# Attention with a softplus layer behind it on one core: in batches 3 to 7 the output matmuls stand two tiles behind h, and sums are placed and split otherwise

## The chip, the cores and the metric

The kernel runs on one core of a Trainium2 chip. The metric is the device time of one execution in microseconds (us). Three runs of the kernel before gave 1178.12, 1180.25 and 1180.36 us; the median is 1180.25 us. A further execution was profiled; the traces and tables here come from it. Engine names in the profile: PE is TensorE (matmuls; PEld are its weight loads), DVE is VectorE, ACT is ScalarE, POOL is GpSimd, SP is SyncE, which issues the DMAs.

## The reference

Eight batches of eight heads; 512 local and 32 global positions of 64 numbers each. A local position attends to the 32 global keys and to local keys within 32 positions; a global position attends to all 544 keys. The rows that come out are the input of a two-layer network with softplus between the layers:

```
s_g = scale * q_g @ concat(k_g, k_l)^T;   out_g = softmax(s_g) @ concat(v_g, v_l)
s_ll = where(|i - j| <= 32, scale * q_l @ k_l^T, -1e9);   s_lg = scale * q_l @ k_g^T
out_l = softmax(concat(s_lg, s_ll)) @ concat(v_g, v_l)
x = concat(out_g, out_l) as (8 * 544, 512)
h = x @ w_in                                   # 512 x 2048
g = max(h, 0) + log1p(exp(-|h|))
out = g @ w_out                                # 2048 x 512
```

All of it is fp32. Each of the two big products is made as three matmuls of rounded high parts and low remainders (high by high, low by high, high by low).

## The kernel before

**Attention.** Work goes by m, a pair of heads (m = 0 to 31, four to a batch). m = 0 to 5 are done ahead of everything, with a scheme of their own. For each m from 6 on there are: `scores` (PE, then DVE adds the mask and `block_maxima` takes maxima of 32 by 32 blocks); `maxima` (`fold` brings four partition groups together with POOL copies, reduces on DVE and copies, then three copies spread the result); `probs`, in two halves (DVE transposes the maxima, POOL subtracts them at L387, ACT takes the exponential at L389, DVE sums blocks at L393); `totals` (`fold` again, reciprocal, three copies, a transpose at L404); `values` (PE) and `normalise` (DVE), which leave x of four m in the tiles xa[b, 0..3]. From m = 9 (`WIDE`) on, `both_scores` does both halves of the scores together: one in the PSUM tile a, the other in both banks of the pool ps_h.

**Batches 0 to 2.** The tile f (16 of them) is 128 of the 2048 columns of h for 512 rows: `hpart` makes h (12 matmuls for the tile, in two parts), `act` makes g (three ACT instructions, e at L695 on DVE, the rounded gh at L698 on ACT, the remainder gl at L700 on POOL), `opart` adds g's product with w_out to the four PSUM banks o0 to o3. Batch 0 shares its time with the weights: they are loaded as 64-bit numbers and split by ACT, DVE and POOL (L575 to L594).

**Batches 3 to 7** (`FAST` = 3) make h by a scheme with seven products where the plain one has eight. It needs sums of blocks of w_in: `mix` makes them once, 16 in all, on POOL (L475, L476), DVE (L477, L479) and ACT (L478), and sends them to a DRAM scratch, from which `load_ring` brings them back in a ring of 12 tiles. It needs sums of blocks of x: `sums_x(b)` makes them on POOL, 14 instructions, and `operand_x(b, i)` splits operand i into high and low (ACT and DVE). A pair p (p = 0 to 7) makes the tiles p and p + 8 of h: `six(b, p)` does six products (36 matmuls) into two PSUM banks of ps_h (in the last batch odd p take the tile a), copying parts to the tile c with ACT; L677 on DVE forms the first h and `act(b, p)` follows; `seventh(b, p)` does the last product (six matmuls), L686 forms the second h, `act(b, p + 8)` follows. `product` frees a ring tile behind odd p, and in pair 7 it calls operand_x for the next batch behind each product. gh and gl have three buffers each, e has two, ps_h two banks.

**What sets the order.** `moe_items` writes a list of items; in batches 3 to 7 a pair stands there as: six, half a tile of o, seventh, half a tile of o, act of the second tile, scores if p is even, a whole tile of o. The o are those of the last tile of the pair before and of the first tile of this pair: o stands one tile behind h. `pieces` gives the attention work slots in units of which a batch has 48; the main loop calls a piece when the items done have reached its slot. Matmuls stay in the order of this program, by `mm`'s chain; the other engines' instructions are put in order by the framework's scheduler, which goes by when it reckons that each is ready. Waits between engines go by semaphores, and each engine runs its own queue in order.

Of the kernel before, what the change touches and what calls it, by code (L numbers as in the profile page):

```python
# [8 lines left out]
F32 = mybir.dt.float32  # L9
# [4 lines left out]
ALU = mybir.AluOpType  # L14
# [5 lines left out]
P = 128  # L20
# [44 lines left out]
def moe_over_global_local_attention(  # L65
# [290 lines left out]

    def fold(t, op):

        for a in range(1, 4):
            nc.gpsimd.tensor_copy(t[0:32, GW * a:GW * a + GW], t[32 * a:32 * a + 32, 0:GW])  # L362
        e0 = 4 * GW
        for u, du, off in ((0, 1, -2), (3, 1, 3)):
            nc.vector.tensor_reduce(grid(t, e0 + u, (7, 6), (du, 2)), grid(t, 3 + u, (12, 6), (du, 2), (off, 2), (GW, 4)), axis=AX.XY, op=op)
        nc.vector.tensor_reduce(grid(t, e0 + 2, (7, 6), (4, 2)), grid(t, 3 + 2, (12, 6), (7, 2), (GW, 4)), axis=AX.X, op=op)
        g = e0 + 44
        nc.vector.tensor_reduce(grid(t, g, (1, 2)), grid(t, 3 + 5, (36, 2), (12, 3), (3, 2), (GW, 4)), axis=AX.XYZ, op=op)
        nc.vector.tensor_copy(grid(t, e0 + 5, (21, 2), (7, 3)), t[0:32, g:g + 2].unsqueeze(2).to_broadcast([32, 2, 3]))
        return t[:, e0:e0 + 44]  # L370

    def maxima(m):
        e = fold(st.pop(("mt", m)), ALU.max)
        for a in range(1, 4):
            i = nc.vector.tensor_copy(e[32 * a:32 * a + 32, 0:42], e[0:32, 0:42]).ins  # L375
        order["maxima"] = i
        st["e", m] = e

    def probs(m, g):
# [14 lines left out]
                                axis=AX.X, op=ALU.add, apply_transpose=True)  # L394

    def totals(m):
        e = fold(st.pop(("zt", m)), ALU.add)
        nc.vector.tensor_scalar(e[0:32, 0:42], e[0:32, 0:42], 1e-9, None, op0=ALU.add)
        nc.vector.reciprocal(e[0:32, 0:42], e[0:32, 0:42])
        for a in (2, 3, 1):  # L400
            o = 21 * (a // 2)
            nc.vector.tensor_copy(e[32 * a:32 * a + 32, 0:21], e[0:32, o:o + 21])
        rb = st["rb", m] = pl.tile([P, 640], F32, tag="rb", name=f"rb{m}", bufs=1)
        nc.vector.transpose(rb.rearrange("p (s k) -> p s k", k=32), e[:, 0:20].unsqueeze(2).to_broadcast([P, 20, 32]))  # L404

# [27 lines left out]
    def pieces():  # L433
        def piece(*fs):
            def go():
                for f in fs:
                    f()
            return go
        ps = []
        for m in range(M0, M):  # L440
            soon = (5, 11.5, 14.7) if m <= 4 * FAST + 4 else (3, 9.5, 13)
            g0, g1, mx, tot, val = SLOTS.get(m, (None, None) + tuple(12 * m + u for u in soon))
            for g, slot in ((0, g0), (1, g1)) if m in SLOTS else ():
                fs = [lambda m=m, g=g: scores(m, g)]
                if m + 1 < M:
                    fs += [lambda m=m, p=p: load(m + 1, p) for p in ((0,), (1, 2))[g]]
                ps.append((slot, piece(*fs)))
            ps.append((mx, piece(lambda m=m: maxima(m), *[lambda m=m, q=q: probs(m, q) for q in range(2)])))
            ps.append((tot, lambda m=m: totals(m)))
            fs = [lambda m=m: values(m), lambda m=m: normalise(m)]  # L450
            if m + 2 < M:
                fs.append(lambda m=m: load_v(m + 2))
            ps.append((val, piece(*fs)))
        for i in range(16):
            ps.append((MIX0 + MIX1 * i, lambda i=i: (mix_out(i), mix(*MIXES[i]))))
        ps.sort(key=lambda t: t[0])
        return ps
# [9 lines left out]
    def mix(q, what):  # L467

        t = mixed
        a11, a12, a21, a22 = wi[2 * q], wi[2 * q + 1], wi[2 * q + 8], wi[2 * q + 9]  # L470
        x, y, op = {"S3": (a11, a21, ALU.subtract), "S1": (a21, a22, ALU.add),
                    "S2": (t.get("S1"), a11, ALU.subtract), "S4": (a12, t.get("S2"), ALU.subtract)}[what]
        o = t[what] = pl.tile([P, 2, 512], F32R, tag="cv", name=f"mix{q}{what}", bufs=2)
        lo = o[:, 1].bitcast(F32)
        nc.gpsimd.tensor_tensor(o[:, 0].bitcast(F32), x[:, 0].bitcast(F32), y[:, 0].bitcast(F32), op=op)  # L475
        nc.gpsimd.tensor_tensor(lo, x[:, 1].bitcast(F32), y[:, 1].bitcast(F32), op=op)  # L476
        nc.vector.tensor_tensor(lo, lo, o[:, 0].bitcast(F32), op=ALU.add)  # L477
        nc.scalar.copy(o[:, 0], lo)  # L478
        nc.vector.tensor_tensor(o[:, 1], lo, o[:, 0].bitcast(F32), op=ALU.subtract)  # L479
# [15 lines left out]
    SECOND = ((lambda t: t[:, 0:128].unsqueeze(1), 0, 1, 128), (lambda t: windows(t, 288, 224, 2, 64), 128, 2, 64))  # L495
    sums, xs = {}, {}

    def sums_x(b):
        t13 = pl.tile([P, 2, 2, 256], F32, tag="cv", name=f"t13_{b}", bufs=2)
        t24 = pl.tile([P, 2, 2, 256], F32, tag="cv", name=f"t24_{b}", bufs=2)  # L500
        t1, t3, t2, t4 = t13[:, 0], t13[:, 1], t24[:, 0], t24[:, 1]
        assert all((b, j) in ready for j in range(4))
        lower, upper = [xa[b, 0], xa[b, 1]], [xa[b, 2], xa[b, 3]]
        for k in range(2):
            cut = lambda t, o, n, w: t[:, k, o:o + n * w].rearrange("p (n w) -> p n w", n=n)
            for f, o, n, w in SECOND:
                a = windows(lower[k], 160 if o == 0 else 384, w, n, w)
                nc.gpsimd.tensor_tensor(cut(t1, o, n, w), f(lower[k]), a, op=ALU.subtract)
                nc.gpsimd.tensor_tensor(cut(t2, o, n, w), f(upper[k]), cut(t1, o, n, w), op=ALU.subtract)  # L509
                nc.gpsimd.tensor_tensor(cut(t3, o, n, w), f(upper[k]), f(lower[k]), op=ALU.subtract)  # L510
            nc.gpsimd.tensor_tensor(cut(t4, 0, 2, 128), half_1(upper[k]), cut(t2, 0, 2, 128), op=ALU.subtract)  # L511
        sums[b] = {5: t1, 6: t2, 7: t3, 4: t4}
# [95 lines left out]
    def moe_items():  # L608
# [46 lines left out]

        def six(b, p):

            if b == B - 1 and p % 2:
                t = ps_a.tile([P, 2, 512], F32, tag="a", name=f"h{b}_{p}")
                t = [t[:, 0], t[:, 1]]  # L660
            else:
                t = [ps_h.tile([P, 512], F32, tag="h", name=f"h{b}_{p}_{u}") for u in range(2)]
            X, N, Q, V = t[0][:, 0:256], t[0][:, 256:512], t[1][:, 0:256], t[1][:, 256:512]
            if "c" not in g:
                g["c"] = pl.tile([P, 2, 512], F32, tag="wi3", name="c", bufs=1)
            c = g["c"]
# [10 lines left out]
            nc.vector.tensor_tensor(c[:, 0], t[1], c[:, 0], op=ALU.add)  # L677
# [70 lines left out]
        for i, (b, f) in enumerate(tiles):  # L748
            if f == 0 and b > 0 and not FAST <= b < B:
                items.append((b, 0, 0, lambda b=b: [split_x(b, j) for j in range(4)]))  # L750
            if FAST <= b < B:
                if f < 8:
                    if f == 7 and b < B - 1:
                        items.append((b, 0, 0, lambda b=b: sums_x(b + 1)))
                    items.append((b, 6, 0, lambda b=b, f=f: six(b, f)))
                    second(done, b)
                    items.append((b, 1, 0, lambda b=b, f=f: seventh(b, f)))
                    second(done + 1, b)
                    items.append((b, 0, 0, lambda b=b, f=f: act(b, f + 8)))
                    m = next(wide, None) if f % 2 == 0 else None  # L760
                    if m:
                        items.append((b, 0, 0, lambda m=m: both_scores(m)))
                    second(done + 2, b)
                    second(done + 3, b)
                    done += 4
                continue
            if 0 < b < B - 1:
                if f == 0:
                    h = iter(range(NF))
                    for what in ORDER:  # L770
                        if what == "H":
# [3 lines left out]
                            if b == FAST - 1 and f % 2 and f > 4:  # L775
                                items.append((b, 0, 0, lambda f=f: (load_ring(f - 5), load_ring(f - 4))))
                            if b == FAST - 1 and f == NF - 1:
                                items.append((b, 0, 0, lambda b=b: sums_x(b + 1)))
                                items.append((b, 0, 0, lambda b=b: [operand_x(b + 1, i) for i in range(7)]))
                        elif what == "O":  # L780
                            second(done, b)
# [175 lines left out]
```

## Time and profile before

| | us |
|---|---|
| median of three runs | 1180.25 |
| the profiled execution | 1181.58 |
| its span, first to last instruction | 1179.80 |
| busy: PE / DVE / ACT / POOL | 994.3 / 760.4 / 567.2 / 550.2 |
| PE idle ahead of o from gh, ended by gh | 96.6 |
| mean granted clock of PE | 0.927 |

Busy times are the union of an engine's instructions; PE's ends are modelled, so that neighbouring matmuls overlap a little in the records, and the price of a step on PE is best read from start to start. "Idle before" is the time in which the engine did nothing ahead of an instruction, with the instruction that ended it. A row of the windows view holds: start:end, length, the busy time of PE, PEld, DVE, ACT and POOL with instruction counts, PE's granted clock (1 is full), the DMA engines' share and GB/s. In the timeline a row holds start, length, engine, line, operation, output and inputs, count, and the idle time ahead of it in brackets. In the waits view a row holds who waited, for whom, total us, times, longest.

Batch 0's h starts at 85 us; the following batches 1 and 2 run to 447 us. The pairs of batch 4 run from 591.7 to 731.5 us, those of batch 5 to 871.4, those of batch 6 to 1004.7, those of batch 7 to 1122.2; the last 58 us are the rows of the global positions.

### The profile page before, as it was taken

To read this page: it belongs to the slowest core of one execution; us is meant where nothing else is said; L and a number is where in the kernel's file an instruction comes from. 1 tells how busy PE (TensorE), PEld (TensorE's weight loads), DVE (VectorE), ACT (ScalarE), POOL (GpSimd) and SP (SyncE) were. 2 spreads that over 40 slices of the span, in tenths; PEclk is the share of its full clock that TensorE was granted. 3 is DMA by queue.
4 is the path that set the end of the run, shared out by engine and by line. 5 is a ranking of instruction groups with operands and counts; after the bars stand their busy time and mean duration, and the time that the engine had idled before them with its cause. 6 is when DMAs were issued, how large, how long until landed. Compare 5 with 4: busy or idle time off the path is not lost. (4 is left out here: it accounts for less than half of the span.)

```text
span 1179.8 us, 16894 instructions
## 1 busy us (share of the span) xinstructions
PE 994.3 (84%) x5955; PEld 810.1 (69%) x5959; DVE 760.4 (64%) x1427; ACT 567.2 (48%) x1086; POOL 550.2 (47%) x736
## 2 busy tenths in 40 slices
PE   6888977789999998888689886888978878788898
PEld 4676755567777787776578765667757666666687
DVE  6889698896676778656876557766675674221211
ACT  6777554544444463443543444444454345444443
POOL 5768889774444453434534334443343452111121
PEclk8999999799999998988899888899888889998999
DMA  9944433331122343344453333544334433433330
GB/s 357 358 148 160 177 97 118 126 112 41 41 79 88 122 152 105 139 154 151 166 201 104 122 134 139 202 166 149 105 137 143 166 126 143 161 125 113 118 127 19
DMA packets 61493, 164.95 MB, mean 140 GB/s; under 512 B 10720, under 2 KB 14560, under 8 KB 61408
## 3 DMA queue, kind: packets, MB, share of 16 engines
q1 hardware_dynamic: 60592, 163.77, 39.6%
q8 instruction: 47, 0.77, 0.3%
q14 instruction: 38, 0.31, 0.1%
q10 hardware_dynamic: 816, 0.10, 0.1%
HBM read 137.63 MB, written 26.21 MB: 139 GB/s over the span
## 5 line engine op out<-in xcount | busy, mean ns | idle before, releaser
L133 PE MATMUL o<-wo,gh 128*128 128x512 f32 x1088 | 383.5, 436 | 100.8 <-ACT gh L698 96.6
L700 POOL TENSOR_TENSOR gl<-e,gh 128x512 fp32r<-128x512 f32 (+1 forms) x152 | 189.0, 1248 | 389.7 <-ACT gh L698 381.7
L133 PEld LDWEIGHTS o<-wo,gh 128*128 128x128 f32 x1088 | 217.6, 210 | 155.8 <-ACT gh L698 108.4
L133 PE MATMUL o<-wo,gl 128*128 128x512 f32 x544 | 239.8, 441 | 31.5 <-POOL gl L700 31.0
L133 PEld LDWEIGHTS o<-wo,gl 128*128 128x128 f32 x544 | 113.8, 209 | 79.4 <-POOL gl L700 53.8
L387 POOL TENSOR_TENSOR s<-s,mb 128x320 f32<-128x320 f32 (+6 forms) x136 | 143.2, 1086 | 49.5 <-DVE mb L383 47.5
L133 PE MATMUL h<-xh,ring 128*128 128x256 f32 x768 | 141.4, 285 | 4.6 <-ACT c L671 2.3
L133 PE MATMUL h<-xh,wi 128*128 128x512 f32 x384 | 122.8, 401 | 12.0 <-DVE e L695 10.8
L133 PEld LDWEIGHTS h<-xh,ring 128*128 128x128 f32 x768 | 122.4, 192 | 11.9 <-ACT c L671 3.1
L698 ACT CAST gh<-e 128x512 fp32r<-128x512 f32 x136 | 83.4, 613 | 89.8 <-DVE e L695 88.3
L677 DVE TENSOR_TENSOR c<-h,c 128x512 f32<-128x512 f32 x40 | 27.0, 676 | 132.2 <-PE h L133 132.2
L133 PE MATMUL h<-xl,ring 128*128 128x256 f32 x384 | 107.5, 280 | 0.0
L133 PE MATMUL h<-x,ring 128*128 128x256 f32 x720 | 99.8, 282 | 6.5 <-ACT c L675 6.3
L133 PEld LDWEIGHTS h<-x,ring 128*128 128x128 f32 x720 | 93.2, 188 | 12.5 <-ACT c L675 8.5
L694 ACT ACTIVATE e<-e,one 128x512 f32<-128x512 f32 x136 | 97.7, 719 | 2.1
L133 PEld LDWEIGHTS h<-xh,wi 128*128 128x128 f32 x384 | 72.2, 191 | 32.3 <-DVE e L695 14.2
L668 ACT COPY c<-h 128x256 f32<-128x256 f32 x40 | 14.9, 371 | 161.4 <-PE h L133 161.4
L393 DVE TRANSPOSE_TENSOR_REDUCE zt<-s 128x32 f32<-128x1024 f32 x52 | 64.6, 1242 | 41.6 <-ACT s L389 41.5
L693 ACT ACTIVATE e<-e 128x512 f32<-128x512 f32 x136 | 85.4, 628 | 2.6
L695 DVE SCALAR_TENSOR_TENSOR e<-c,e 128x512 f32<-128x512 f32 x80 | 64.8, 810 | 26.8 <-ACT e L694 23.9
L692 ACT ACTIVATE e<-c 128x512 f32<-128x512 f32 x80 | 50.2, 628 | 59.3 <-DVE c L677 54.9
L133 PE MATMUL h<-xl,wi 128*128 128x512 f32 x192 | 76.2, 397 | 0.0
(193 smaller groups left out, 1607.4 us busy)
## 6 DMA issues: line engine op xcount, KB each, us to landing
ring<-mix_scratch SPq DMA_DIRECT2D x156, 512.0 KB, 5.7
raw<-in_qk SPq DMA_DIRECT2D x52, 272.0 KB, 3.0
v<-in_v SPq DMA_DIRECT2D x26, 384.0 KB, 3.1
wiraw<-in_w_in SPq DMA_DIRECT2D x16, 512.0 KB, 9.0
woraw<-in_w_out SPq DMA_DIRECT2D x16, 512.0 KB, 9.0
mix_scratch<-wi SPq DMA_DIRECT2D x16, 512.0 KB, 5.4
out<-ot SPq DMA_DIRECT2D x29, 256.0 KB, 2.1
raw<-in_qk SPq DMA_DIRECT2D x26, 224.0 KB, 3.4
```

What stands on the lines that cost most here:

```text
L133: order["pe"] = after(nc.tensor.matmul(*a, **k), "pe").ins
L387: nc.gpsimd.tensor_tensor(s[:, h, o:o + w], s[:, h, o:o + w], mb[:, h, q:q + w], op=ALU.subtract)
L393: nc.vector.tensor_reduce(windows(st["zt", m], 4 + 16 * g, 36, 2, 16), s.rearrange("p h (b k) -> p h b k", k=32), axis=AX.X, op=ALU.add, a ...
L668: nc.scalar.copy(c[:, 0, 0:256], X)
L677: nc.vector.tensor_tensor(c[:, 0], t[1], c[:, 0], op=ALU.add)
L692: nc.scalar.activation(e, ph, AF.Abs)
L693: nc.scalar.activation(e, e, AF.Exp, scale=-1.0)
L694: nc.scalar.activation(e, e, AF.Ln, bias=one)
L695: nc.vector.scalar_tensor_tensor(e, ph, 0.0, e, op0=ALU.max, op1=ALU.add)
L698: nc.scalar.copy(gh, e)
L700: nc.gpsimd.tensor_tensor(gl[:, c], e[:, c], gh[:, c].bitcast(F32), op=ALU.subtract)
```

## The change

In batches 3 to 7 a pair becomes: six, half a tile of o, seventh, half a tile of o, act of the second tile, scores if p is even, a whole tile of o, where the o are now those of both tiles of the pair before. `sums_x` makes half of its sums ahead of pair 6, half ahead of pair 7. In the last batch all pairs use ps_h. The second half of `probs` has a slot of its own, 1.5 later, for m over 16, and the slots of the m that are divisible by four lie later. In `mix` two additions go from DVE to POOL, and the slots of its 16 calls begin later and lie closer together. The small copies of `fold`, `maxima` and `totals` go from DVE to ACT for m = 6, 7 and 8, and the splitting of the weights is no longer ordered behind the maxima of those m. e (L695) stays on DVE.

```diff
-MIX0, MIX1 = 104, 4
+MIX0, MIX1 = 110, 3.6
...
+    def small(m):
+        return nc.scalar.copy if m < WIDE else nc.vector.tensor_copy
...
-        nc.vector.tensor_copy(grid(t, e0 + 5, (21, 2), (7, 3)), t[0:32, g:g + 2].unsqueeze(2).to_broadcast([32, 2, 3]))
+        small(m)(grid(t, e0 + 5, (21, 2), (7, 3)), t[0:32, g:g + 2].unsqueeze(2).to_broadcast([32, 2, 3]))
...
         for a in range(1, 4):
-            i = nc.vector.tensor_copy(e[32 * a:32 * a + 32, 0:42], e[0:32, 0:42]).ins
-        order["maxima"] = i
+            i = small(m)(e[32 * a:32 * a + 32, 0:42], e[0:32, 0:42]).ins
+        if m >= WIDE:
+            order["maxima"] = i
...
-            nc.vector.tensor_copy(e[32 * a:32 * a + 32, 0:21], e[0:32, o:o + 21])
+            small(m)(e[32 * a:32 * a + 32, 0:21], e[0:32, o:o + 21])
...
-            soon = (5, 11.5, 14.7) if m <= 4 * FAST + 4 else (3, 9.5, 13)
+            soon = (5, 11.5, 14.7) if m <= 4 * FAST + 4 else (3, 9.5, 13) if m % 4 else (7, 13, 16)
...
-            ps.append((mx, piece(lambda m=m: maxima(m), *[lambda m=m, q=q: probs(m, q) for q in range(2)])))
+            ps.append((mx, piece(lambda m=m: maxima(m), lambda m=m: probs(m, 0))))
+            ps.append((mx + (1.5 if m > 4 * FAST + 4 else 0), lambda m=m: probs(m, 1)))
...
-        nc.vector.tensor_tensor(lo, lo, o[:, 0].bitcast(F32), op=ALU.add)
+        nc.gpsimd.tensor_tensor(lo, lo, o[:, 0].bitcast(F32), op=ALU.add)
         nc.scalar.copy(o[:, 0], lo)
-        nc.vector.tensor_tensor(o[:, 1], lo, o[:, 0].bitcast(F32), op=ALU.subtract)
+        nc.gpsimd.tensor_tensor(o[:, 1], lo, o[:, 0].bitcast(F32), op=ALU.subtract)
...
-    def sums_x(b):
+    def sums_x(b, k):
...
-        for k in range(2):
-            cut = lambda t, o, n, w: t[:, k, o:o + n * w].rearrange("p (n w) -> p n w", n=n)
-            for f, o, n, w in SECOND:
-                a = windows(lower[k], 160 if o == 0 else 384, w, n, w)
+        lower, upper = xa[b, k], xa[b, k + 2]
+        cut = lambda t, o, n, w: t[:, k, o:o + n * w].rearrange("p (n w) -> p n w", n=n)
+        for f, o, n, w in SECOND:
+            a = windows(lower, 160 if o == 0 else 384, w, n, w)
...
-            if b == B - 1 and p % 2:
-                t = ps_a.tile([P, 2, 512], F32, tag="a", name=f"h{b}_{p}")
-                t = [t[:, 0], t[:, 1]]
-            else:
-                t = [ps_h.tile([P, 512], F32, tag="h", name=f"h{b}_{p}_{u}") for u in range(2)]
+            t = [ps_h.tile([P, 512], F32, tag="h", name=f"h{b}_{p}_{u}") for u in range(2)]
...
-                    if f == 7 and b < B - 1:
-                        items.append((b, 0, 0, lambda b=b: sums_x(b + 1)))
+                    if f in (6, 7) and b < B - 1:
+                        items.append((b, 0, 0, lambda b=b, k=f - 6: sums_x(b + 1, k)))
                     items.append((b, 6, 0, lambda b=b, f=f: six(b, f)))
-                    second(done, b)
-                    items.append((b, 1, 0, lambda b=b, f=f: seventh(b, f)))
-                    second(done + 1, b)
-                    items.append((b, 0, 0, lambda b=b, f=f: act(b, f + 8)))
-                    m = next(wide, None) if f % 2 == 0 else None
-                    if m:
-                        items.append((b, 0, 0, lambda m=m: both_scores(m)))
-                    second(done + 2, b)
-                    second(done + 3, b)
-                    done += 4
+                    late = 2 * tiles.index((b, f)) - done
+                    assert late == 4 or (b, f) == (FAST, 0) and late <= 4, (b, f, late)
+                    k = iter(range(done, done + late))
+                    for step in "OHOAGOO":
+                        if step == "O":
+                            k0 = next(k, None)
+                            if k0 is not None:
+                                second(k0, b)
+                                done += 1
+                        elif step == "H":
+                            items.append((b, 1, 0, lambda b=b, f=f: seventh(b, f)))
+                        elif step == "A":
+                            items.append((b, 0, 0, lambda b=b, f=f: act(b, f + 8)))
+                        elif f % 2 == 0:
+                            m = next(wide, None)
+                            if m:
+                                items.append((b, 0, 0, lambda m=m: both_scores(m)))
```

`second(i, b)` puts half a tile of o, the i-th of the list, into the items.

More of the change, by code (lines that the diff above doesn't have):

```diff
@@ L355, in grid, with fold @@
         return bass.AP(base.tensor, base.offset, [list(base.ap[0])] + [list(d) for d in dims])
-    def fold(t, op):
+    def small(m):
+        return nc.scalar.copy if m < WIDE else nc.vector.tensor_copy
+    def fold(t, op, m):
         for a in range(1, 4):
@@ L368, in fold @@
         nc.vector.tensor_reduce(grid(t, g, (1, 2)), grid(t, 3 + 5, (36, 2), (12, 3), (3, 2), (GW, 4)), axis=AX.XYZ, op=op)
-        nc.vector.tensor_copy(grid(t, e0 + 5, (21, 2), (7, 3)), t[0:32, g:g + 2].unsqueeze(2).to_broadcast([32, 2, 3]))
+        small(m)(grid(t, e0 + 5, (21, 2), (7, 3)), t[0:32, g:g + 2].unsqueeze(2).to_broadcast([32, 2, 3]))
         return t[:, e0:e0 + 44]
     def maxima(m):
-        e = fold(st.pop(("mt", m)), ALU.max)
+        e = fold(st.pop(("mt", m)), ALU.max, m)
         for a in range(1, 4):
-            i = nc.vector.tensor_copy(e[32 * a:32 * a + 32, 0:42], e[0:32, 0:42]).ins
-        order["maxima"] = i
+            i = small(m)(e[32 * a:32 * a + 32, 0:42], e[0:32, 0:42]).ins
+        if m >= WIDE:
+            order["maxima"] = i
         st["e", m] = e
@@ L396, in totals @@
     def totals(m):
-        e = fold(st.pop(("zt", m)), ALU.add)
+        e = fold(st.pop(("zt", m)), ALU.add, m)
         nc.vector.tensor_scalar(e[0:32, 0:42], e[0:32, 0:42], 1e-9, None, op0=ALU.add)
@@ L496, in moe_over_global_local_attention @@
     sums, xs = {}, {}
-    def sums_x(b):
[L499 to L503, printed above, removed]
-        for k in range(2):
-            cut = lambda t, o, n, w: t[:, k, o:o + n * w].rearrange("p (n w) -> p n w", n=n)
-            for f, o, n, w in SECOND:
-                a = windows(lower[k], 160 if o == 0 else 384, w, n, w)
[L508 to L512, printed above, removed]
+    def sums_x(b, k):
+        if k == 0:
+            t13, t24 = (pl.tile([P, 2, 2, 256], F32, tag="cv", name=f"{n}_{b}", bufs=2) for n in ("t13", "t24"))
+            sums[b] = {5: t13[:, 0], 6: t24[:, 0], 7: t13[:, 1], 4: t24[:, 1]}
+        t1, t2, t3, t4 = (sums[b][i] for i in (5, 6, 7, 4))
+        assert (b, k) in ready and (b, k + 2) in ready
+        lower, upper = xa[b, k], xa[b, k + 2]
+        cut = lambda t, o, n, w: t[:, k, o:o + n * w].rearrange("p (n w) -> p n w", n=n)
+        for f, o, n, w in SECOND:
+            a = windows(lower, 160 if o == 0 else 384, w, n, w)
+            nc.gpsimd.tensor_tensor(cut(t1, o, n, w), f(lower), a, op=ALU.subtract)
+            nc.gpsimd.tensor_tensor(cut(t2, o, n, w), f(upper), cut(t1, o, n, w), op=ALU.subtract)
+            nc.gpsimd.tensor_tensor(cut(t3, o, n, w), f(upper), f(lower), op=ALU.subtract)
+        nc.gpsimd.tensor_tensor(cut(t4, 0, 2, 128), half_1(upper), cut(t2, 0, 2, 128), op=ALU.subtract)
     def operand_x(b, i):
@@ L777, in moe_items @@
                             if b == FAST - 1 and f == NF - 1:
-                                items.append((b, 0, 0, lambda b=b: sums_x(b + 1)))
+                                items.append((b, 0, 0, lambda b=b: [sums_x(b + 1, k) for k in range(2)]))
                                 items.append((b, 0, 0, lambda b=b: [operand_x(b + 1, i) for i in range(7)]))
```

## The prediction

> **What bounds the kernel now.** I read the page first, for the tile that TensorE (PE) idles in front of; then the busy times by stage, to see where that idling lies; then the waits of one batch and TensorE's timeline, for its price.
>
> ```profile
> PE 994.3 (84%) x5955; PEld 810.1 (69%) x5959; DVE 760.4 (64%) x1427; ACT 567.2 (48%) x1086; POOL 550.2 (47%) x736
> L133 PE MATMUL o<-wo,gh 128*128 128x512 f32 x1088 | 383.5, 436 | 100.8 <-ACT gh L698 96.6
> ```
>
> PE is the busiest engine, and 100.8 us of idle time stand ahead of one group, the output matmuls o, which wait for gh, the softplus of h rounded by ScalarE (ACT). By stage (the columns are PE, PE's weight loads, VectorE = DVE, ACT, GpSimd = POOL, then PE's granted clock): five rows are batches 3 to 7, one each; the last two are batch 0 and batch 1.
>
> ```profile
> 451.00:591.70 140.70, 113.10 (x705) 93.48 (x705) 100.19 (x203) 63.46 (x118) 64.84 (x91) 0.88 0.42 147
> 591.70:731.50 139.80, 114.67 (x738) 95.19 (x738) 93.78 (x187) 62.11 (x118) 58.47 (x82) 0.89 0.42 148
> 731.50:871.40 139.90, 114.63 (x738) 95.21 (x737) 93.73 (x187) 62.13 (x118) 58.47 (x82) 0.89 0.43 148
> 871.40:1004.70 133.30, 111.34 (x709) 92.75 (x708) 77.82 (x157) 60.03 (x116) 49.64 (x68) 0.91 0.40 141
> 1004.70:1122.20 117.50, 94.59 (x518) 77.50 (x516) 28.59 (x37) 52.88 (x101) 17.93 (x14) 0.94 0.38 133
> 85.00:195.00 110.00, 95.74 (x440) 73.07 (x444) 94.46 (x142) 64.76 (x108) 96.29 (x109) 0.97 0.43 154
> 195.00:321.00 126.00, 103.60 (x534) 81.84 (x529) 98.92 (x176) 54.74 (x87) 76.28 (x88) 0.93 0.23 81
> ```
>
> In batches 3 to 7 nothing is full: PE is busy 115 of 140 us at a clock of 0.89, DVE 94. So it is a chain of latencies. The waits of batch 4 (window 591.7 to 731.5) name it: the four gh waits end with PE idle, the next four are DVE's own.
>
> ```profile
> PE o L133 <- ACT gh L698: 21.5, 4, 7.8
> DVE c L677 <- PE h L133: 17.8, 4, 4.9
> PE o L133 <- POOL gl L700: 2.4, 4, 0.6
> DVE zt L365 <- POOL zt L362: 6.8, 4, 2.0
> DVE zt L393 <- ACT s L389: 5.1, 6, 1.3
> DVE mt L365 <- POOL mt L362: 3.8, 4, 1.0
> DVE e L695 <- ACT e L694: 2.0, 6, 0.4
> ```
>
> PE's timeline through two pairs of that batch (start, length) gives the price of every step:
>
> ```profile
> 652.60 1.22 PE L133 MATMUL o<-wo,gh 128*128 128x512 f32 x2 [4.28 <-ACT gh L698]
> ...
> 658.90 0.63 PE L133 MATMUL h<-xh,ring 128*128 128x256 f32 x2
> ...
> 664.79 0.86 PE L133 MATMUL h<-x,ring 128*128 128x256 f32 x6
> 665.49 0.62 PE L133 MATMUL o<-wo,gh 128*128 128x512 f32 x2
> ...
> 666.98 2.21 PE L133 MATMUL s_ps<-raw 64*128 64x160 f32 x28
> 669.11 0.73 PE L133 MATMUL o<-wo,gh 128*128 128x512 f32 x2
> ...
> 672.20 1.96 PE L133 MATMUL v_ps<-s,v 128*64 128x160 f32 x24
> 674.09 0.51 PE L133 MATMUL h<-xh,ring 128*128 128x256 f32 x2
> ...
> 678.45 0.63 PE L133 MATMUL o<-wo,gh 128*128 128x512 f32 x2
> ...
> 679.85 0.39 PE L133 MATMUL h<-x,ring 128*128 128x256 f32 x2
> ```
>
> From start to start: six() 4.36 us (674.09 to 678.45), half a tile of o 1.40 (678.45 to 679.85), seventh() 0.70 (664.79 to 665.49), scores 2.13 (666.98 to 669.11), a whole tile of o behind them 3.09, values 1.89. The tile of o at 652.60 took 6.30 us to the start of six() at 658.90: after a 4.28 us gap its matmuls run at half pace (two in 1.22 us against 0.62). Less its gl wait of about 0.6, that is 5.7 against 2.8, so 2.9 us lost on top of the gap.
>
> **The change, part by part.** *o two tiles behind h (batches 3 to 7).* Before, o of the tile that six() made comes after half an o, seventh() and half an o: 1.40 + 0.70 + 1.40 = 3.5 us (more with scores and values). Now a whole tile of o and the next six() lie between as well: 3.5 + 2.8 + 4.36 = 10.65 us, and 14.7 in pairs with scores and values. The same count of matmuls is issued; only their order moves. What must fit is the time from six()'s end until gl is written:
>
> ```profile
> 1009.22 0.69 DVE L677 TENSOR_TENSOR c<-h,c 128x512 f32<-128x512 f32 x1 [9.66 <-PE h L133]
> ...
> 1014.53 1.28 POOL L700 TENSOR_TENSOR gl<-e,gh 128x512 fp32r<-128x512 f32 x1 [12.61 <-ACT gh L698]
> ```
>
> ```profile
> 687.08 1.79 POOL L700 TENSOR_TENSOR gl<-e,gh 128x512 fp32r<-128x512 f32 x1 [2.76 <-ACT gh L698]
> ```
>
> ```profile
> 712.92 0.63 PE L133 MATMUL o<-wo,gh 128*128 128x512 f32 x2
> ...
> 725.83 1.28 POOL L700 TENSOR_TENSOR gl<-e,gh 128x512 fp32r<-128x512 f32 x1 [4.03 <-ACT gh L698]
> ```
>
> Without attention around it (batch 7) the chain takes 1014.53 + 1.28 - 1009.22 = 6.6 us, hidden. In a pair without scores it took 687.08 + 1.79 - 678.45 = 10.4, because maxima and probs stand ahead on DVE and ACT: just hidden. At the end of a batch (operand_x for the next one in the way) 727.11 - 712.92 = 14.2: about 3.5 us stay open. Three gh buffers suffice: when seventh()'s gh is written, the oldest tile's o has been issued.
>
> If PE alone decides, two pairs take 2 x (4.36 + 0.70) + 4 x 1.40 + 3.09 + 2.8 + 2.13 + 1.89 = 25.6 us, a batch 102.5. The other way: 139.8 - 21.5 - 2.4 - 4 x 2.9 = 104.3. So about 103.
>
> What is late next is DVE. Its 93.8 us of work in batch 4 stay (e stays there too), and it runs in order. Its waits for PE go when PE runs ahead; those for POOL and ACT, 6.8 + 5.1 + 3.8 + 2.0 = 17.7, I keep whole, though probs' second half, moved 1.5 slots later, may shorten them. That makes 111.5, more than 103, so DVE sets batches 3 to 5: 100.2 + 17.7 = 117.9, 111.5 and 111.4, a gain of 22.8 + 28.3 + 28.5. Batch 6 has three scores left: DVE 77.8 + 3/4 of 17.7 = 91, PE 3 x 25.6 + 2 x 10.65 = 98.1, plus 3.5 at the boundary = 101.6: 31.7 gained. Batch 7 has none: 8 x 10.65 + 3.5 = 88.7 against 117.5: 28.8. ACT (52.9 of 88.7) is not full.
>
> *The clock.* The forecast lets the short waits that DVE imposes cost nothing beyond themselves. This row pair of batch 7 speaks against that:
>
> ```profile
> 1027.50:1031.00 3.50, 1.87 (x7) 0.87 (x6) 1.58 (x3) 2.96 (x5) 1.05 (x1) 1.00 1.00 408
> 1031.00:1034.50 3.50, 3.22 (x8) 2.55 (x9) 0.77 (x1) 0.62 (x1) 1.50 (x2) 0.56 0.03 11
> ```
>
> PE was busy 1.87 of 3.50 us, with no gap as long as 1.7, and the clock of the next 3.5 us was 0.56. So two short gaps close together can cost up to 1.5 us more. If that happened once in every two pairs of batches 3 to 6, it would be 16 x 1.5 = 24 us; I keep it for the range. [...]
>
> *sums_x split.* Its 14 instructions for a batch stay; half go ahead of the pair 6, half ahead of pair 7. POOL is busy 58 of 140 us: nothing, and with 112 it still has room.
>
> *The scores' 4th map later; the last batch's odd h in ps_h.* The first takes DVE work out of the boundary, inside the 3.5 us that I left there. The second lets six() of batch 7 take two banks; its short waits for copies of c are inside the 28.8.
>
> *mix and small copies (batches 0 and 1).*
>
> ```profile
> L477 DVE TENSOR_TENSOR mix0S<-mix0S 128x512 f32<-128x512 f32 x4 | 3.6, 890 | 2.5 <-POOL mix0S L476 2.5
> L479 DVE TENSOR_TENSOR mix1S<-mix1S 128x512 fp32r<-128x512 f32 x4 | 5.0, 1258 | 0.2
> L475 POOL TENSOR_TENSOR mix2S<-wi,wi 128x512 f32<-128x512 f32 x2 | 2.6, 1290 | 0.0
> L375 DVE COPY mt<-mt 32x42 f32<-32x42 f32 x21 | 6.3, 298 | 0.4
> L531 ACT CAST x<-xa 128x128 fp32r<-128x128 f32 x4 | 0.9, 304 | 0.0
> ```
>
> 32 additions leave DVE, eight groups of four at 3.6 to 5.0 us (29 to 40 us), and go to POOL at 1.29: 41 us more. POOL was busy 96.3 + 76.3 of the 236 us of batches 0 and 1; 214 of 236 still fits, but its queue also holds gl and the weights' low halves. 24 copies of about 0.30 us (m = 6, 7, 8) go from DVE to ACT, busy 64.8 of 110: nothing. From the waits of 80 to 265:
>
> ```profile
> PE o L133 <- POOL gl L700: 12.8, 4, 8.0
> PE h L133 <- DVE e L695: 7.8, 6, 1.8
> ```
>
> The best case takes away both, 20.6 us; the worst adds the 41 us of POOL to PE's path. DVE's relief and POOL's load pull against each other in the same queues: I take 0 and keep both ends. [...]
>
> Sum: 22.8 + 28.3 + 28.5 + 31.7 + 28.8 = 140. The profiled execution took 1181.6 us (span 1179.8 and 1.8 around it), 1.3 above the median of the runs: 1181.6 - 140 = 1041.6, so 1040 for the median.
>
> **The rivals.** (a) *PE sets all five batches*, because DVE's waits dissolve: batches 3 to 5 at 103, the rest as above: 178 saved with batches 6 and 7 at 98 and 85; about 1003. For it: DVE has 94 of 103. Against: that is 91% in order. (b) *DVE keeps its wait for PE too*, because L677 is queued ahead of work that is ready: batches 3 to 5 cost 17.8 more each, 1040 + 53 = 1093. For it: L677 held DVE up to 4.9 us. Against: with PE ahead there is less to wait for. (c) *POOL holds up batches 0 and 1*: 20 to 41 us late, about 1070. (d) *Slower*: scores' second half takes both h banks, which L677 and L686 must have left; both stand in DVE's queue behind maxima and probs. If two pairs then settle at 36 us, six() and scores waiting in turn for DVE, four batches cost 4 x 4 more than their 140: 1180 + 16 = 1196. It decides once DVE needs over 35 us for two pairs; 94/4 + 17.7/4 = 28 speaks against it. (e) *The change does not do what it says*: the third gh buffer is not free in time and the copy into gh waits instead of o: 1180.
>
> **How the numbers follow.** Forecast 0.52, (a) 0.22, (b) 0.10, (c) 0.09, (d) 0.03, (e) 0.04. Within 0.2% (2.4 us, about what a measurement of this kernel can tell): 0.04; slower 0.03; faster 0.93. The range goes from (a), 1000, to a little below (b), 1088, and takes in the clock's 24 us and POOL's 41.
>
> **What would show it.** Right: in the windows of batches 4 and 5 the gh wait of PE falls from 21.5 to under 5 us, the clock rises from 0.89 to 0.95 or more, DVE is over 80% busy, a batch takes about 112 us, batch 7 under 92. Wrong: PE's waits there are replaced by waits for c (L677, L686) or for gh at the end of pairs without scores; or PE waits for gl before 320 us more than 12.8.

## The result, and the profile after

The changed kernel took 1030.23 us (median of four runs, 1028.71 to 1031.42) against 1179.18 for the kernel before (1177.34 to 1180.36): a ratio of 0.8737, with a 95% interval of 0.8719 to 0.8756. The forecast was 1040, with a range of 1000 to 1088. The profiled execution took 1028.71 us, its span 1026.9.

The page of the changed kernel: the busy times, and the two groups of output matmuls with the idle time ahead of them.

```profile
PE 937.2 (91%) x5955; PEld 786.5 (77%) x5959; DVE 729.3 (71%) x1371; ACT 573.9 (56%) x1110; POOL 584.0 (57%) x768
L133 PE MATMUL o<-wo,gh 128*128 128x512 f32 x1088 | 349.2, 402 | 7.9 <-ACT wo L597 4.2
L133 PE MATMUL o<-wo,gl 128*128 128x512 f32 x544 | 218.5, 402 | 12.9 <-POOL gl L701 12.9
```

Ahead of o from gh, 100.8 us of idle time became 7.9, and gh itself is no longer named there. The same matmuls are also shorter, 402 ns in the mean for 436: in both profiles one takes from 387 to 796 ns, and fewer of them run at half pace (the mean granted clock is 0.977 for 0.927). The windows of the changed kernel, batches 3 to 7 and then everything from batch 0's first h to batch 3's (columns as before: window, length, PE, PEld, DVE, ACT, POOL, granted clock, DMA share, GB/s):

```profile
446.90:556.80 109.90, 101.82 (x726) 88.92 (x725) 94.95 (x195) 59.56 (x113) 61.34 (x87) 0.98 0.53 188
556.80:668.50 111.70, 103.60 (x738) 89.67 (x737) 92.98 (x187) 62.41 (x119) 59.05 (x83) 1.00 0.52 185
668.50:780.20 111.70, 103.55 (x738) 89.58 (x737) 92.90 (x187) 62.42 (x119) 58.99 (x83) 1.00 0.53 185
780.20:888.00 107.80, 102.49 (x709) 89.20 (x708) 86.22 (x175) 64.32 (x123) 52.56 (x74) 0.98 0.47 166
888.00:973.30 85.30, 85.30 (x535) 76.58 (x535) 30.50 (x39) 54.52 (x104) 22.09 (x18) 1.00 0.53 195
85.00:446.90 361.90, 324.48 (x1661) 257.94 (x1662) 256.55 (x449) 185.58 (x319) 260.69 (x312) 0.96 0.33 110
```

Measured alike, from a batch's first h to the next one's, the lengths are these (us):

| batch | before | after | saved | forecast of the saving |
|---|---|---|---|---|
| 3 | 144.5 | 109.9 | 34.6 | 22.8 |
| 4 | 139.8 | 111.7 | 28.1 | 28.3 |
| 5 | 139.9 | 111.7 | 28.2 | 28.5 |
| 6 | 133.4 | 107.9 | 25.5 | 31.7 |
| 7 | 124.2 | 85.3 | 38.9 | 28.8 |
| the rest behind | 50.8 | 53.6 | -2.8 | |

Batches 0 to 2 end where they did, at 447 us. The 2.8 us at the end are one tile of o that now falls behind batch 7 instead of into batch 3. Batch 7's length before contains the last pair's late o, which the prediction's window left out; its window of batch 3 began 4 us later than this one.

What TensorE still waits for in batch 4 of the changed kernel is all but 0.2 us of its idle time there. Of it 3.9 us lie in pair 0, behind the end of batch 3, 2.2 in pair 7, and 0.7 and 1.2 in the pairs 2 and 6. The waits, and the timeline at the batch's end and just behind it:

```profile
PE h L133 <- ACT c L669: 3.8, 3, 1.9
PE h L133 <- ACT c L672: 1.9, 2, 1.0
PE h L133 <- ACT c L676: 1.1, 1, 1.1
PE h L133 <- DVE c L687: 1.1, 1, 1.1
```

```profile
659.99 0.98 PE L133 MATMUL h<-x,ring 128*128 128x256 f32 x6 [1.00 <-ACT c L672]
663.50 0.98 PE L133 MATMUL h<-x,ring 128*128 128x256 f32 x6 [1.15 <-ACT c L676]
670.50 0.51 PE L133 MATMUL h<-xh,ring 128*128 128x256 f32 x2 [1.14 <-DVE c L687]
674.01 0.50 PE L133 MATMUL h<-xh,ring 128*128 128x256 f32 x2 [1.83 <-ACT c L669]
676.59 0.98 PE L133 MATMUL h<-x,ring 128*128 128x256 f32 x6 [0.90 <-ACT c L672]
```

Batch 4 ends at 668.5, so the last three rows are pair 0 of batch 5; in pair 0 of batch 4 the gaps are 1.14, 1.87 and 0.90 us. The new waits are for the copies of c, which take the first products out of PSUM, and for L687, which frees the other bank: products, not outputs, are what TensorE stands in front of now. The pairs of batch 4 take 17.5, 12.5, 15.7, 10.6, 15.2, 10.6, 16.4 and 13.2 us, where the prediction's prices give 14.7 for a pair with scores and values and 10.65 for one without. Pair 0 holds scores without values and pair 1 values without scores; in the run without softmax below they take 12.7 and 12.5. So 4.8 us are lost in pair 0 and 2.7 in pair 7, none in the pairs 1, 3 and 5. Before, they took 15.4, 18.5, 14.9, 18.6, 15.2, 19.3, 14.9 and 23.1.

### The profile page after: what moved, and what is told of

Same layout as the page of the kernel before. It is cut to its first block, busy times and chain, and to the rows that moved or that the text cites. A ratio compares the mean times of both kernels' runs of the same rounds, so it can differ in the third digit from the quotient of the medians.

```text
span 1026.9 us, 16894 instructions
## 1 busy us (share of the span) xinstructions
PE 937.2 (91%) x5955; PEld 786.5 (77%) x5959; DVE 729.3 (71%) x1371; ACT 573.9 (56%) x1110; POOL 584.0 (57%) x768
## 5 line engine op out<-in xcount | busy, mean ns | idle before, releaser
L133 PE MATMUL o<-wo,gh 128*128 128x512 f32 x1088 | 349.2, 402 | 7.9 <-ACT wo L597 4.2
L701 POOL TENSOR_TENSOR gl<-e,gh 128x512 fp32r<-128x512 f32 (+1 forms) x152 | 185.1, 1223 | 218.6 <-ACT gh L699 203.8
L133 PEld LDWEIGHTS o<-wo,gh 128*128 128x128 f32 x1088 | 199.9, 191 | 50.5 <-ACT wo L597 4.7
L133 PE MATMUL o<-wo,gl 128*128 128x512 f32 x544 | 218.5, 402 | 12.9 <-POOL gl L701 12.9
L133 PEld LDWEIGHTS h<-xh,ring 128*128 128x128 f32 x768 | 120.2, 190 | 27.7 <-ACT c L669 14.1
L133 PEld LDWEIGHTS o<-wo,gl 128*128 128x128 f32 x544 | 104.1, 191 | 39.3 <-POOL gl L701 15.1
L133 PE MATMUL h<-x,ring 128*128 128x256 f32 x720 | 101.5, 285 | 9.1 <-ACT c L672 5.3
L133 PEld LDWEIGHTS h<-x,ring 128*128 128x128 f32 x720 | 94.1, 191 | 15.4 <-ACT c L672 6.7
L695 ACT ACTIVATE e<-e,one 128x512 f32<-128x512 f32 x136 | 98.0, 720 | 2.7
L133 PEld LDWEIGHTS h<-xh,wi 128*128 128x128 f32 x384 | 73.2, 193 | 29.5 <-DVE e L696 11.3
L398 DVE TRANSPOSE_TENSOR_REDUCE zt<-s 128x32 f32<-128x1024 f32 x52 | 64.5, 1241 | 38.2 <-ACT s L394 37.8
L696 DVE SCALAR_TENSOR_TENSOR e<-c,e 128x512 f32<-128x512 f32 x80 | 69.9, 874 | 25.2 <-ACT e L695 22.6
L696 DVE SCALAR_TENSOR_TENSOR e<-h,e 128x512 f32<-128x512 f32 x56 | 38.0, 679 | 63.4 <-ACT e L695 57.7
L693 ACT ACTIVATE e<-h 128x512 f32<-128x512 f32 x56 | 33.3, 594 | 83.1 <-PE h L133 72.1
```

Of the source, the lines that this page charges most:

```text
L133: order["pe"] = after(nc.tensor.matmul(*a, **k), "pe").ins
L398: nc.vector.tensor_reduce(windows(st["zt", m], 4 + 16 * g, 36, 2, 16), s.rearrange("p h (b k) -> p h b k", k=32), axis=AX.X, op=ALU.add, a ...
L693: nc.scalar.activation(e, ph, AF.Abs)
L695: nc.scalar.activation(e, e, AF.Ln, bias=one)
L696: nc.vector.scalar_tensor_tensor(e, ph, 0.0, e, op0=ALU.max, op1=ALU.add)
L701: nc.gpsimd.tensor_tensor(gl[:, c], e[:, c], gh[:, c].bitcast(F32), op=ALU.subtract)
```

## The experiments

The theory at the start: o's slack is the whole gain, and VectorE then sets batches 3 to 5. The rivals: the other edits are needed for it; or TensorE sets those batches, and only the queues at the end of a batch cost more.

**The order alone, and everything but the order.** First the kernel before with the new list of items only:

```diff
-                    second(done, b)
-                    items.append((b, 1, 0, lambda b=b, f=f: seventh(b, f)))
...
+                    late = 2 * tiles.index((b, f)) - done
+                    k = iter(range(done, done + late))
+                    for step in "OHOAGOO":
...
```

> The kernel before with the new order of items alone: o two tiles behind h, everything else as before. Theory (the gain is the slack that o gets, 10.65 us where it had 3.5): 1030 to 1040 us, PE's wait for gh in batch 4 gone from 21.5 us to under 2. Rival (the gain needs the relief of VectorE too: probs split, slots of every fourth m, sums_x split, additions and copies moved): 1050 to 1080 us, with PE waiting for c or gh at the end of each batch for over 12 us.

It took 1037.97 us (0.8800, 0.8777 to 0.8823). In its batch 4 TensorE waits for no gh:

```profile
PE h L133 <- ACT c L668: 3.1, 2, 1.9
PE h L133 <- ACT c L675: 1.2, 1, 1.2
PE h L133 <- DVE c L686: 1.1, 1, 1.1
PE h L133 <- ACT c L671: 1.0, 1, 1.0
```

Its batches 3 to 6 take 111.1, 111.1, 110.7 and 106.8 us, 1.5 us less in all than in the changed kernel: there the split of probs and of sums_x and the later slots bring nothing. Only batch 7 differs, 96.7 us for 85.3.

The other way round, the changed kernel with the old list of items (the diff above, reversed; `sums_x` stays split):

> The changed kernel with the old order of items: o one tile behind h, everything else as changed. Theory: 1170 to 1182 us, with PE's wait for gh in batch 4 still near 21.5 us. Rival (probs split and sums placed otherwise shorten the chain to gh): 1100 to 1150 us.

It took 1161.73 us (0.9853, 0.9819 to 0.9888), faster than the theory said and far from the rival. In its batch 4 the waits are nearly those of before:

```profile
PE o L133 <- ACT gh L699: 19.7, 4, 7.8
PE o L133 <- POOL gl L701: 2.4, 4, 0.6
PE h L133 <- ACT c L676: 1.1, 1, 1.1
```

Batches 4 and 5 come out 3.1 and 3.3 us shorter than before, batch 6 3.6, batch 7 14.4, batch 3 1.5 longer. So under the old order the other edits are worth some 17 us, and on top of the new one 8.

**The order and the last batch's banks.** The order alone, plus ps_h for all pairs of batch 7:

```diff
-            if b == B - 1 and p % 2:
-                t = ps_a.tile([P, 2, 512], F32, tag="a", name=f"h{b}_{p}")
-                t = [t[:, 0], t[:, 1]]
-            else:
-                t = [ps_h.tile([P, 512], F32, tag="h", name=f"h{b}_{p}_{u}") for u in range(2)]
+            t = [ps_h.tile([P, 512], F32, tag="h", name=f"h{b}_{p}_{u}") for u in range(2)]
```

> The kernel before with the new order of items and with ps_h for all pairs of the last batch, nothing else. Against the run with the order alone, batch 7 should fall from 96.7 to 85.3 us: 1026 to 1029 us, the time of the changed kernel or a little less, if the other edits are worth nothing. Rival (the other edits carry part of it): 1032 to 1038 us.

1027.50 us (0.8717, 0.8690 to 0.8744); batch 7 takes 85.2. These two edits carry the whole gain of the change. With the tile a, the order alone left these waits in odd pairs of batch 7 (its timeline, one pair):

```profile
899.12 0.51 PE L133 MATMUL h<-xh,ring 128*128 128x256 f32 x2 [0.46 <-ACT c L668]
901.23 0.50 PE L133 MATMUL h<-xh,ring 128*128 128x256 f32 x2 [0.46 <-ACT c L671]
903.64 0.98 PE L133 MATMUL h<-x,ring 128*128 128x256 f32 x6 [0.74 <-ACT c L675]
```

Each copy of c out of one bank stops the next product although that one goes to the other bank. The even pairs of the same run, whose banks are two tiles, have no such wait. That two slices of one tile are taken as one is a likely reason; no run shows it apart.

**Half the step.** The changed kernel with o one tile and a half behind:

```diff
-                    late = 2 * tiles.index((b, f)) - done
+                    late = 2 * tiles.index((b, f)) - done + 1
```

> The changed kernel with o one tile and a half behind h: the first half of the tile that six() makes is the last o of its own pair, so it comes 1.40 + 0.70 + 1.40 + 1.40 = 4.9 us behind six() where it came 3.5 us in the old order and comes 10.65 us in the new one (scores, 2.1 us, lie between in every other pair). The chain to gh takes 8.6 us in pairs without scores, to gl 10.4. Theory (slack is what counts, us for us): the gap of 4.3 us there shrinks to about 2.5 to 3, in batch 7 to nothing; 1090 to 1120 us. Rival (a threshold: any gap is nearly as dear as the whole, as it halves the clock): 1130 us or more. Rival (half a tile is enough): under 1050 us.

1115.03 us (0.9463, 0.9441 to 0.9485), inside the theory's range. Its batch 4:

```profile
PE o L133 <- ACT gh L699: 13.5, 4, 6.4
PE o L133 <- POOL gl L701: 3.2, 3, 1.2
```

The run to compare it with is the one with the old order and the same other edits: the four gh waits fall from 19.7 to 13.5 us. The longest, at the batch's end, falls from 7.8 to 6.4, just the 1.4 us of half a tile of o; the other three from 11.9 to 7.1, 1.6 each. Batch 4 is 6.6 us shorter (136.8 to 130.2), a little more than four times 1.4; its clock is 0.92 for 0.90. Batch 7 has 0.3 us of waits for gh left: it takes 95.2 us, with 5.0 us of waits for gl. Slack counts about us for us.

**Does VectorE set batches 3 to 6?** Two runs, one with more work for it and one with less. More: block maxima twice for 12 of the m.

```diff
-        block_maxima(m, 0)
-        block_maxima(m, 1)
+        for _ in range(2 if m > 4 * FAST + 4 and m % 4 else 1):
+            block_maxima(m, 0)
+            block_maxima(m, 1)
```

> The changed kernel with the block maxima of 12 of the m of batches 3 to 6 (17 to 31 without those divisible by four) taken twice, the same result again: 24 instructions of 1.24 us = 30 us more on VectorE, in pairs that do not end a batch. If VectorE sets the time of batches 3 to 6, as the prediction has it: 1055 to 1062 us. Rival (in those pairs TensorE sets it, and only the queues at the end of a batch cost time): 1029 to 1036 us.

1047.30 us (0.8876, 0.8853 to 0.8900): 17 us dearer, between the two. But the 30 us did not arrive. L341 takes 28.6 us more (64.4 to 93.0), while the e of batches 3 to 7 (L696, here L697) takes 6.1 less (69.9 to 63.8), and VectorE's busy time rose by 17.9 us in all, from 729.3 to 747.2. What was added to its busy time cost about us for us. The pairs 3 and 5 of batch 4 (10.6 us) did not move; the pairs with scores took the cost, in part as longer waits for c: in batch 4 TensorE waits 10.8 us for 7.9. Less: the small copies on ScalarE for every m.

```diff
-        return nc.scalar.copy if m < WIDE else nc.vector.tensor_copy
+        return nc.scalar.copy
...
-        if m >= WIDE:
-            order["maxima"] = i
```

> The changed kernel with the small copies of fold, maxima and totals on ScalarE for every m, not just for 6, 7 and 8: about 8.3 us of VectorE a batch (3.6 + 2.0 + 2.7 in batch 4 before) go to ScalarE, busy 62 of 112. If VectorE sets the time: 1000 to 1012 us. Rival (VectorE has slack except at the end of a batch): 1026 to 1032 us. If ScalarE's queue in front of the copies of c is what counts there: 1032 to 1045 us.

1026.21 us (0.8693, 0.8660 to 0.8725), 4 us less than the changed kernel. But that came from batches 0 to 2 (h of batch 3 starts at 443.8 us); its batches 4 and 5:

```profile
553.80:666.40 112.60, 105.85 (x737) 91.93 (x736) 86.95 (x155) 68.30 (x150) 59.61 (x82) 0.97 0.53 183
666.40:779.00 112.60, 105.56 (x737) 91.69 (x736) 86.91 (x155) 68.30 (x150) 59.59 (x82) 0.97 0.53 184
```

VectorE is 6 us less busy a batch (86.9 for 93.0), ScalarE 6 more, and the batch is 0.9 us longer. This does not clear VectorE. The pairs 2, 4 and 6 fell from 15.7, 15.2 and 16.4 us to 14.9 each, TensorE's own price, and the pairs 0, 3, 5 and 7 rose by 3.6 us together: VectorE now waits 9.5 us for ScalarE in place of 5.7, and the granted clock of either batch is 0.97 for 1.00. Work moved from one engine to the next in the same chain is not work taken away. And ScalarE with more work of its own, gh rounded twice in the middle pairs:

```diff
             nc.scalar.copy(gh, e)
+            if FAST <= b < B - 1 and 2 <= f % 8 <= 5:
+                nc.scalar.copy(gh, e)
```

> The changed kernel with the rounding to gh done twice, the same result again, for the tiles of pairs 2 to 5 of batches 3 to 6: 8 casts of 0.61 us, 4.9 us a batch more on ScalarE, 20 us in all. If those pairs are set by TensorE and o's slack covers the rest: 1029 to 1033 us. If the queue of ScalarE (gh waiting for e, copies of c behind it) sets them: 1040 to 1050 us.

1035.17 us (0.8774, 0.8752 to 0.8796), 5 us dearer for 20 us of work, just over the range of the first reading and far under the second. Batches 4 and 5 cost 0.8 and 0.6 us more, batch 3 3.7. So ScalarE's total is not the bound. For VectorE, its own waits in batch 4 of the changed kernel (556.8 to 668.5) say more:

```profile
DVE zt L369 <- POOL zt L366: 6.4, 4, 2.1
DVE zt L398 <- ACT s L394: 4.0, 4, 1.3
DVE mt L369 <- POOL mt L366: 3.8, 4, 1.0
DVE e L696 <- ACT e L695: 1.7, 4, 0.7
DVE s L335 <- PE s_ps L133: 1.0, 2, 0.7
```

The waits for GpSimd and ScalarE are still 15.9 us of the 17.7 before, those for TensorE are down to 1.0. Together with 93.0 us of work they fill 109.9 of the 111.7 us: VectorE has next to no slack in such a batch, and TensorE, idle for 8.1 us, has little.

**The end of a batch.** First by order: operand_x for the next batch behind all of six().

```diff
-            if p == 7 and b < B - 1:
+            if p == 7 and b < B - 1 and i == 6:
                 operand_x(b + 1, i)
...
             g["X"] = X
+            for i in range(6 if p == 7 and b < B - 1 else 0):
+                operand_x(b + 1, i)
             act(b, p)
```

> The changed kernel with six of the seven operand_x for the next batch called behind six() of pair 7 and not behind each product, so that the copies of c do not stand behind their casts in ScalarE's queue. Theory (the queues at the end of a batch cost the 5 to 8 us of TensorE's waits for c): 1010 to 1022 us. Rival (the same work of ScalarE and VectorE then holds up the next pair instead): 1027 to 1034 us.

1031.67 us (0.8754, 0.8732 to 0.8775), no gain. The wait for L676 falls from 1.15 to 0.64 us at that place, the one for the second bank (L689 here) grows from 1.14 to 1.80: as the rival said, the work is moved and not removed. The scheduler still puts casts of operand_x between the copies of c, so this run changed less than the edit reads. Then by leaving work out, with no softmax steps (maxima, probs, totals) for any m over 16:

```diff
+            if m > 4 * FAST + 4:
+                ps.append((tot, lambda m=m: no_softmax(m)))
+            else:
...
```

> The changed kernel without maxima, probs and totals for m over 16: the scores go into values as they are, so the output is not the reference's; scores, masks, block maxima, values and normalise stay. Over 9 us of GpSimd, 2 us of ScalarE and some 11 us of VectorE go for each of these m. If the softmax steps are what lies in front of the copies of c and of L687 at the end of a batch: batches 4 and 5 take 102 to 105 us, TensorE's own time, and the whole 990 to 1000 us. Rival (operand_x and the sums of x hold up the end of a batch by themselves): batches of 107 to 110 us, 1010 to 1022 us in all.

996.96 us (0.8452, 0.8431 to 0.8474). Batches 4 and 5 run without one wait of TensorE:

```profile
555.90:657.40 101.50, 101.50 (x738) 89.25 (x737) 54.50 (x87) 55.77 (x111) 30.99 (x38) 1.00 0.58 203
657.40:758.70 101.30, 101.30 (x737) 89.06 (x736) 54.40 (x87) 55.68 (x111) 30.97 (x38) 1.00 0.58 202
```

101.5 us is TensorE's own price of such a batch, and operand_x and the sums of x, which are all still there, cost nothing by themselves. Last, softmax left out for m = 20, 24 and 28 only, the three that meet operand_x (the edit against the run just shown):

```diff
-            if m > 4 * FAST + 4:
+            if m > 4 * FAST + 4 and m % 4 == 0:
```

> The changed kernel without maxima, probs and totals for m = 20, 24 and 28 alone, the three whose softmax meets operand_x at the end of batches 3, 4 and 5; their scores go into values as they are, so the output is not the reference's. Without softmax for any m over 16 the gain was 33 us. Theory (the time lost is where softmax and operand_x meet in the queues): three batch ends of some 7 us each, 1006 to 1012 us, more than half of the gain with a quarter of the work left out, batch 4 at 104 us. Rival (VectorE's load over the whole batch sets it): a fifth to a quarter of the gain, 1021 to 1025 us, batch 4 at 109.

1009.77 us (0.8565, 0.8537 to 0.8594): 20 of the 33 us for three of the fifteen m. Batch 4:

```profile
557.60:661.90 104.30, 102.23 (x737) 89.42 (x736) 81.68 (x161) 60.42 (x117) 51.31 (x71) 1.00 0.56 198
```

Its pairs 0 and 7 fall from 17.5 and 13.2 us to 12.7 and 10.5; the pairs 2, 4 and 6 stay at 15.7, 15.2 and 16.4, as in the changed kernel. So 7.4 of the 10.2 us that batch 4 loses to TensorE's price lie where the softmax of one m meets operand_x, and the rest lies in the other pairs with scores. The edit also takes 11.3 us of VectorE's work out of batch 4 (93.0 to 81.7), after which the prediction's sum would let TensorE set it too. For the place, and against the total, speaks that the pairs 2, 4 and 6 did not move; a run without the softmax of one m in the middle of a batch, which would decide it, is missing.

**Batches 0 to 2.** The changed kernel with mix as before:

```diff
-MIX0, MIX1 = 110, 3.6
+MIX0, MIX1 = 104, 4
...
-        nc.gpsimd.tensor_tensor(lo, lo, o[:, 0].bitcast(F32), op=ALU.add)
+        nc.vector.tensor_tensor(lo, lo, o[:, 0].bitcast(F32), op=ALU.add)
...
-        nc.gpsimd.tensor_tensor(o[:, 1], lo, o[:, 0].bitcast(F32), op=ALU.subtract)
+        nc.vector.tensor_tensor(o[:, 1], lo, o[:, 0].bitcast(F32), op=ALU.subtract)
```

> The changed kernel with mix as before: its two additions on VectorE, its slots as before. If relief of VectorE and load of GpSimd cancel, as the prediction took it: 1028 to 1033 us, h of batch 3 starting at 447 us within 2. Rival (GpSimd's load costs): 1015 to 1025 us. Rival (VectorE's relief gains): 1036 to 1050 us.

1026.55 us (0.8710, 0.8689 to 0.8732), a little under the range of the first reading; its interval overlaps that of the changed kernel. h of batch 3 starts at 444.3 us. Over all profiles it starts at 447.0 to 448.3 with neither edit (three kernels), at 446.9 to 449.7 with both (eight), at 444.3 and 443.4 with the copies on ScalarE and mix left on VectorE (two). So the moved copies (with the order of the weights' splitting, which goes with them) gain some 4 us, the moved additions and later slots of mix lose about as much, and they cancel.

**A version that beats both.** Order, banks, and the copies on ScalarE for m up to 16 (the splitting of the weights no longer ordered behind the maxima of those m), with mix, sums_x, probs and the slots as before:

```diff
+    def small(m):
+        return nc.scalar.copy if m <= 4 * FAST + 4 else nc.vector.tensor_copy
```

> The kernel before with the new order of items, ps_h for all pairs of the last batch, and the small copies on ScalarE for m up to 16; mix, sums_x, probs and the slots as before. From the runs so far: batches 3 to 7 as with order and banks (525 us), batches 0 to 2 some 3 us shorter than there: 1022 to 1026 us, faster than the changed kernel. Rival (the copies gain only beside the moved mix): 1026 to 1029 us.

1023.67 us (median of five, 0.8683, 0.8658 to 0.8707); the interval lies below that of the changed kernel. Against order and banks alone (0.8690 to 0.8744) the intervals overlap.

## Why the prediction was right

**o two tiles behind h: right.** By itself it takes 141 of the 149 us, gh's wait in batch 4 goes from 21.5 us to nothing, and half the step gives back the part that its slack pays for. The chain at the end of a batch (14.2 us to gl for 10.65 of slack) was expected to leave 3.5 us open in front of o. No wait of o for gh or gl is left there; TensorE comes later there, stopped by other waits.

**TensorE's price of 103 us a batch: right.** Without softmax a batch takes 101.5, against 102.5 from the starts and 104.3 from the waits. In the changed kernel batch 4 is 103.6 us busy at a clock of 1.00.

**"DVE sets batches 3 to 5": the sum held in batches 4 and 5, the rule did not.** Its 111.5 us met the 111.7 measured, and its terms are found again: 93.0 us busy for 93.8, 15.9 of waits for 17.7. The same rule gave 117.9 for batch 3, which took 109.9: the waits there came to 10.6 us. It let TensorE set batch 6 at 101.6, which took 107.9: VectorE is busy 86.2 us there and not 77.8, since more of its work now falls into that batch (175 instructions for 157). And the price of its work depends on the place. Pairs without scores and values inside the batch run at TensorE's price of 10.6 us, while most of the time is lost at the end of a batch, where the softmax of an m and operand_x stand in VectorE's and ScalarE's queues ahead of L687 and the copies of c. The changed kernel's queue of VectorE at that place:

```profile
666.77 3.06 DVE L537 TENSOR_TENSOR x<-xa,x 128x128 fp32r<-128x128 f32 x4
669.76 0.68 DVE L687 TENSOR_TENSOR c<-h,c 128x512 f32<-128x512 f32 x1
670.36 0.68 DVE L530 TENSOR_TENSOR x<-t,x 128x512 fp32r<-128x512 f32 x1
670.96 1.23 DVE L398 TRANSPOSE_TENSOR_REDUCE zt<-s 128x32 f32<-128x1024 f32 x1
672.12 0.64 DVE L696 SCALAR_TENSOR_TENSOR e<-c,e 128x512 f32<-128x512 f32 x1
```

And ScalarE's:

```profile
670.47 0.63 ACT L693 ACTIVATE e<-c 128x512 f32<-128x512 f32 x1 [1.49 <-DVE c L687]
671.01 0.71 ACT L695 ACTIVATE e<-e,one 128x512 f32<-128x512 f32 x1
671.63 1.04 ACT L394 ACTIVATE s<-s 128x1024 f32<-128x1024 f32 x1
672.57 0.61 ACT L694 ACTIVATE e<-e 128x512 f32<-128x512 f32 x1
673.09 0.60 ACT L699 CAST gh<-e 128x512 fp32r<-128x512 f32 x1
673.60 0.36 ACT L669 COPY c<-h 128x256 f32<-128x256 f32 x1
```

On VectorE four subtractions of operand_x (L537) stand ahead of L687, and ScalarE, whose next instruction needs L687, stands still for 1.49 us. Another one (L530) and the softmax's block sums (L398) stand ahead of the e (L696) of the first tile of pair 7, which is the last to read that half of c. The copy at 673.60 is the one for which TensorE stood idle for 1.83 us. Its product was done at 669.4, but there is one tile c, and L696 read the half that it writes until 672.8; from then on it stood 0.8 us behind the next tile's exponential and gh. So the copy of c waits until the e of that tile is made, and whatever stands in the two queues ahead of that e delays it.

The prediction's view could not show this: it added up VectorE's busy time and its waits for others over a batch, and such a sum does not tell where in the batch they fall. Rival (a) had VectorE's waits dissolve; in batch 4 nearly all of them stayed, and its 1003 us was missed.

That the total came within 10 us owes something to luck: batch 3 saved 11.8 us more than forecast, batch 7 10.1 more, batch 6 6.2 less, and the rest behind cost 2.8. Two of the signs of being wrong came up as well: TensorE's waits for gh were replaced by waits for c (7.9 us in batch 4, L687, which was L686, among them), and before 320 us TensorE waits 12.9 us for gl, where the line was 12.8.

**The later slots for every fourth m: wrong.** They were to take VectorE's work out of the batch's end. The softmax of m = 24 still lies there: its two exponentials start 1.07 us ahead of the end of batch 4 and 3.14 behind it, with the order alone 1.07 ahead and 3.13 behind. Leaving it out gave 7 us a batch. The scheduler, which goes by when it reckons work ready, is a likely reason why the slot did not move it; no run shows it.

**Batch 7: right in kind, wrong in size.** The banks were to be "inside the 28.8". They are a term of their own: 96.7 us without them, 85.3 with, against 8 times 10.65 = 85.2. Without them the order alone would have stood at 1038, closer to the forecast than the change itself.

**mix and the copies: right.** 0 with both ends kept; two effects of some 4 us against each other.

**The clock: right to keep apart.** The 24 us feared from pairs of short gaps did not come: a clock of 1.00 in batches 4, 5 and 7, of 0.98 in batches 3 and 6.

**The rivals.** (b), (d) and (e) fell: the addition that was L677 (now L678) does not wait for TensorE at all in batch 4, nothing is slower, and gh waits for its buffer once in batches 3 to 7, for 0.9 us. (c) fell in size.

## What to carry to other kernels

When the engine that should be busy waits for the end of a chain, count the time from the start of that chain to its use, and compare it with the longest the chain takes anywhere, not with its mean: here 6.6, 10.4 and 14.2 us stood against 3.5 of slack. Give it another step of slack before you shorten the chain. Then look where in the period the next waits fall; an engine's busy time and waits, added up, tell that it has no slack, but not which of its work is dear. That is told by the place where another engine stands still for it, here a short copy that frees a bank, behind work that could have come later.

## What the runs showed of the hardware

Gaps of like length were followed by different clocks. Behind batch 4 of the changed kernel gaps of 1.14, 1.83 and 0.90 us left the clock at 1.00; behind batch 5 gaps of 1.14 and 1.86 us were followed by 3.41 us at 0.50. The last two rows are the 3.41 us ahead of the moment at which the clock fell, 786.03 us, and the 3.41 us behind it; the first two lie one batch, 111.70 us, earlier:

```profile
670.92:674.33 3.41, 1.58 (x13) 1.37 (x12) 3.02 (x4) 3.41 (x7) 0.56 (x1) 1.00 0.00 0
674.33:677.74 3.41, 2.51 (x20) 2.26 (x19) 2.37 (x6) 1.70 (x5) 3.08 (x5) 1.00 0.00 0
782.62:786.03 3.41, 1.55 (x13) 1.35 (x12) 3.02 (x4) 3.41 (x7) 0.56 (x1) 1.00 0.00 0
786.03:789.44 3.41, 3.41 (x17) 3.23 (x16) 2.37 (x7) 1.79 (x5) 3.06 (x5) 0.50 0.00 0
```

TensorE was busy 1.55 us of the stretch ahead of the half clock and 1.58 us of the one that left the clock alone; the longest gaps differ by 0.03 us as well. What decides between the two, no run shows.

An addition of 128 by 512 in two SBUF inputs, moved from VectorE to GpSimd, took 1.28 to 1.43 us there in the mean of each group against 0.89 to 1.26 before; what sets the groups apart was not measured.
